# A second tile pool in a fused attention and gated-convolution kernel: every tile that TensorE reads gets one base address mod 256 bytes

## The chip, the core and the metric

The kernel runs on one core of one Trainium2 chip. The metric is device time in microseconds (us) of one execution, as the median of several runs. "Before" is the kernel without the change. Engines are called as the profile calls them: PE is TensorE's matmul side, PEld its weight load, DVE is VectorE, ACT is ScalarE, POOL is GpSimd, SP is the engine that issues the DMAs.

## What is computed

An attention between 512 tokens and 32 state vectors per head, both ways, whose two results are laid one behind the other along the sequence (544 rows), and on that a projection to 1024 columns, a convolution of three taps along the sequence, a gate, and a projection back. All in float32; B = 8, H = 8, D = 64.

```python
def attn(x, state):                              # x (8,8,512,64), state (8,8,32,64)
    a  = softmax(x @ state.T / 8)                # 512 x 32 for each head
    a2 = softmax(state @ x.T / 8)                # 32 x 512 for each head
    return concat([a @ state, a2 @ x], axis=2)   # 544 rows

def block(x, w_in, conv_w, w_out):               # x is (8, 544, 512) now
    h = maximum(x @ w_in, 0)                     # (8, 544, 1024)
    c = sum(conv_w[k] * shifted(h, k - 1) for k in range(3))
    return (h * sigmoid(c)) @ w_out              # (8, 544, 512)
```

## The kernel before

The work goes in eight batches `b`, and for each in eight slices `f` of 128 of the 1024 middle columns, which gives 64 steps `i`. The projection into the middle is not done as attention result times `w_in`: the state is multiplied by `w_in` first (`state_product`, L494, tile `u`), and a step is then `u` against the attention weights `a` (`hidden`, L579, out `ps_h`). ACT takes it out of PSUM through ReLU into `h` (L584), ACT and DVE make the three taps into `t` (L601, L605, L610), ACT the tanh of the gate (L614), DVE the gated product (L619). Then `t` is multiplied by `w_out` into four chunks of 128 rows (`project`, L637, out `acc`), which collect over the eight steps of a batch and are copied out by ACT or DVE (L651, L653) and stored. The 32 state rows of each batch go the same way in groups of four batches (`ps_hs`, `ss`, `gts`, `acc_t`), and one corner chunk is done late (`last`, `acc_c`).

Most products are done in a split form. A float32 tile is written by ACT as a rounded part (`high`, L178, type fp32r) and by DVE as the rest (`low`, L181), so the pairs `a0`, `a1`; `u0`, `u1`; `g0`, `g1`; the two halves of `wo`; `gts0`, `gts1` and the two parts of `last` come about. One product is then three fp32r matmuls of 512 columns: `PASSES = ((1, 0), (0, 1), (0, 0))`, rest times rounded, rounded times rest, rounded times rounded. In a matmul one operand is loaded as weights (128 columns) and the other streams by. In `project`, `tail` and `last_product`, all on L637, the slices of `g`, `gts` and `last` are loaded and `wo` streams; in `hidden`, `u` is loaded and `a` streams. The first batch and four of its steps run in plain float32, without a split (L574, L645).

`ORDER` is a table of numbers that sets the order of all operations by hand, on all engines; operations are not scheduled otherwise. What each waits for follows from the tiles that it reads and writes, and from how many buffers a tag has (`SBUF`).

Tiles of SBUF come from two pools. `keep` holds what stays for the whole run, in this order: `ident`, `cw`, `wi`, `wo`, `st`, `sr`, the 16 small `hs`, three `corner` tiles, `last`. `work` holds everything that is used in turn, through `buf` (L159 of before), a ring of buffers for each tag. The pools lie one behind the other in each partition, and in a pool the tags lie in the order in which they are first asked for, each rounded up to 32 bytes. So a tile whose size is no multiple of 256 bytes moves all that come after it to another place mod 256.

These are the places of the tiles in a partition, as the built program has them, mod 256 bytes. No base but those of the small tiles and of `h` differs within one row.

```
tile                       bytes     before   after
ident                        512        128     128
wi, wo, st, sr          2048-32768      224     128
last                        4096        192     128
xt, hc, at                2048-4096      192     128
a0 (streams in hidden)      4096         64     128
a1 (streams in hidden)      4096        192     128
u0 (loaded in hidden)       4096        192     128
u1 (loaded in hidden)       4096         64     128
the two parts of last       4096        192     128
xx, e2t, rr             512-4096        192     128
af, e2, t                2048-4096       64     128
g0, g1, gts0, gts1, ss     512-2048      64     128
o (copied out)              2048         64     128
h                           2052   192,224,0,32   192,224,0,32
hs, cw, corner, nm2, s1, s2   up to 544 bytes, at many places, the same mod 256 in both
```

`a0`, `a1` and `u1` share their buffers with `raw`, the tiles into which the weights are loaded at the start, and four of the last outputs share those of `xt` and `e2`.

Of the kernel before, what the change touches and what calls it, by code (L numbers as in the profile page):

```python
# [9 lines left out]
F32 = mybir.dt.float32  # L10
F32R = mybir.dt.float32r
# [4 lines left out]
P = 128  # L16
B, H, S, NS, D = 8, 8, 512, 32, 64
NP = H // 2
NG = H // 4
NCH = S // P  # L20
DM, DFF = 512, 1024
NK = DM // P
NF = DFF // P
T = S + NS

LOTS = ((0, 1, 2, 3), (4, 5, 6, 7))
# [16 lines left out]

SBUF = dict(hc=3, xt=4, xx=2, at=5, e2=2, e2t=2, af=1, a=2, u=2, h=4, t=5, g=4, ss=1,
            rr=2, nm2=4, s2=4, s1=4, o=2, gts=2)

RAW = ("a0", "a1", "u1")
PSUM = dict(acc=4, ph=2, ps=2)
# [103 lines left out]
def fused_kernel(ctx: ExitStack, tc: tile.TileContext, xT, xn, stT, w_in, conv_w, w_out, out):  # L152
    nc = tc.nc
    V, A, G, PE = nc.vector, nc.scalar, nc.gpsimd, nc.tensor

    psum = ctx.enter_context(tc.tile_pool(name="psum", bufs=4, space=bass.MemoryType.PSUM))
    keep = ctx.enter_context(tc.tile_pool(name="keep", bufs=1))
    work = ctx.enter_context(tc.tile_pool(name="work", bufs=2))

    def bank(name, tag="ps"):  # L160
        return psum.tile([P, 512], F32, tag=tag, name=name, bufs=PSUM[tag])

    def buf(shape, dtype, tag, name, pool=work, **kw):
        return pool.tile(shape, dtype, tag=tag, name=name, bufs=SBUF.get(tag) or SBUF[tag[:-1]], **kw)

    ident = keep.tile([P, P], F32, name="ident")
    make_identity(nc, ident)
    cw = keep.tile([P, NF, 3], F32, name="cw")
    wi = keep.tile([P, NK, DFF], F32, name="wi")
    wo = keep.tile([P, 2, NF, DM], F32R, name="wo")  # L170

    st = keep.tile([P, B * NP, NS], F32, name="st")

    sr = [keep.tile([P, NP, len(lot) * NS], F32, name=f"sr_{m}") for m, lot in enumerate(LOTS)]


    def high(hi, src):
# [24 lines left out]
    def w_tile(j, tag, *more):  # L202
        shape = [P, *pieces[j][0].shape[1:], *more]
        return buf(shape, U32, tag, f"{'raw' if more else tag}_{j}",
                   padded_shape=[P, *([1, 512] if j == W_CONV else shape[1:3]), *more])
# [18 lines left out]
    def w_sign(j):  # L224
        dst = pieces[j][1]
        if dst is None:
            f = j - W_OUT
            whole[f] = buf([P, DM], F32, f"g{f % 2}", f"whole_{f}")
            dst = whole[f].unsqueeze(1)
        V.scalar_tensor_tensor(dst.bitcast(U32), raws.pop(j)[:, :, :, 1], 0x80000000, hcs.pop(j),  # L230
                               op0=ALU.bitwise_and, op1=ALU.bitwise_or)
# [27 lines left out]
    at, ps_s, nm2, e2, ps_t, e2t, s2, ps_r, rr, ps_f, xts, xxs = ({} for _ in range(12))  # L259

    def xt_load(i):
        b, g = divmod(i, NG)
        xts[i] = buf([P, 2, S], F32, "xt", f"xt_{i}")
        nc.sync.dma_start(xts[i], xT[b, :, 2 * g:2 * g + 2, :])  # L264
# [99 lines left out]
    af, s1, av = {}, {}, {}  # L364
# [182 lines left out]
    corner = keep.tile([P, NF, 3], F32, name="corner")  # L547
    corner2 = keep.tile([P, NF, 3], F32, name="corner2")
    corners = keep.tile([P, 1, NF], F32, name="corners")
    last = keep.tile([P, NF, P], F32, name="last")  # L550

    def at_step(i):
        b, f = divmod(i, NF)
# [326 lines left out]
```

## Time and profile before

| | us |
|---|---|
| median of 3 runs | 376.81 |
| lowest and highest of them | 375.97, 378.32 |
| the profiled execution's own time | 376.16 |
| its span, first to last instruction | 374.4 |
| PE busy | 362.8 |
| DVE busy | 309.2 |
| ACT busy | 265.7 |
| POOL busy | 44.2 |

The granted clock of TensorE in the profiled execution was 0.996 of full speed. Busy time is the time that instructions of an engine cover, and PE's counts a matmul up to its modelled end, so that back-to-back matmuls overlap: the length of one matmul in a row is longer than the step from one to the next. The step is read from the chain of waits, which lists pieces of uninterrupted work with their length and the number of instructions in each.

### The profile page before, as it was taken

The page shows a single profiled execution, that of the slowest core. Times are in us where ns is not written, and L with a number is a line of the kernel's source. Part 1 is how long each engine was busy: PE and PEld are TensorE (multiplying, and loading weights), DVE is VectorE, ACT ScalarE, POOL GpSimd, SP SyncE. Part 2 cuts the span into 40 slices and gives each one's busy share as a digit, 9 for nine tenths or more (in the row PEclk, how much of TensorE's full clock was granted, in tenths as well). Part 3 has the DMA queues.
Part 4 walks back from the last instruction along what each step waited for, and adds up shares of the span by engine and source line. Part 5 has one row for each costly group of instructions (what it writes and reads, how often), then busy time and mean ns, then how long its engine had stood idle before and what let it go on. Part 6 is the DMA issues. An engine that isn't in the chain of part 4 may idle for free.

```text
span 374.4 us, 6509 instructions
## 1 busy us (share of the span) xinstructions
PE 362.8 (97%) x2418; PEld 267.4 (71%) x2418; DVE 309.2 (83%) x540; ACT 265.7 (71%) x536; POOL 44.2 (12%) x158
## 2 busy tenths in 40 slices
PE   7988989999999999999999999999999999999994
PEld 6852446677668776877888877877778778888883
DVE  1988999999999989989989898786787578666951
ACT  3898998866789689766765658666766477558632
POOL 1002102310121120102010011011311121011000
PEclk9999999999999999999999999999999999999998
DMA  7999984033310445000010011100020001002004
GB/s 257 326 355 312 379 290 166 0 114 100 141 43 2 144 141 190 34 2 4 28 56 2 0 56 58 56 4 15 13 86 0 28 30 56 2 0 86 3 0 168
DMA packets 21728, 35.05 MB, mean 94 GB/s; under 512 B 1600, under 2 KB 14272, under 8 KB 21696
## 3 DMA queue, kind: packets, MB, share of 16 engines
q1 hardware_dynamic: 21696, 34.63, 27.0%
q8 instruction: 19, 0.31, 0.4%
q14 instruction: 13, 0.11, 0.1%
HBM read 25.71 MB, written 8.91 MB: 92 GB/s over the span
## 4 chain that ended last, share of the span: by engine, by line
PE 89%; DMA 7%; SPq 2%; ACT 0%; issue 0%; ACTq 0%
PE acc L637 45%; PE ps_h L579 21%; PE ps_hs L560 4%; PE ps_u L494 4%; PE acc_t L637 3%; DMA raw<-w_in 3%; DMA st<-stT 3%; PE ps_h L574 2%; PE acc L645 2%; PE ps_r L318 2%; PE ps_s L277 2%; DMA xx<-xn 2%; PE acc_c L637 1%; PE ps_t L305 1%; SPq L209 1%; SPq L264 0%
## 5 line engine op out<-in xcount | busy, mean ns | idle before, releaser
L637 PE MATMUL acc<-wo,g 128*128 128x512 f32 x708 | 179.9, 400 | 0.0
L637 PEld LDWEIGHTS acc<-wo,g 128*128 128x128 f32 x708 | 131.0, 188 | 43.3 <-issue 8.4
L579 PE MATMUL ps_h<-a,u 128*128 128x512 f32 x336 | 85.7, 397 | 0.0
L579 PEld LDWEIGHTS ps_h<-a,u 128*128 128x128 f32 x336 | 62.4, 188 | 15.9 <-issue 1.7
L605 DVE SCALAR_TENSOR_TENSOR t<-h,cw,t 128x511 f32<-128x511 f32 x64 | 47.1, 744 | 11.0 <-ACT t L601 10.8
L584 ACT ACTIVATE h<-ps_h 128x512 f32<-128x512 f32 x64 | 37.8, 594 | 19.6 <-PE ps_h L579 12.9
L614 ACT ACTIVATE t<-t 128x512 f32<-128x512 f32 x64 | 39.6, 627 | 15.3 <-DVE t L610 15.2
L610 DVE SCALAR_TENSOR_TENSOR t<-h,cw,t 128x512 f32<-128x512 f32 (+1 forms) x64 | 47.3, 745 | 1.7 <-POOL h L589 0.5
L619 DVE SCALAR_TENSOR_TENSOR t<-t,h 128x512 f32<-128x512 f32 (+1 forms) x64 | 42.2, 666 | 5.8 <-ACT t L614 5.6
L181 DVE TENSOR_TENSOR g<-t,g 128x512 fp32r<-128x512 f32 (+1 forms) x60 | 40.2, 674 | 7.4 <-ACT g L178 7.1
L178 ACT ACTIVATE g<-t 128x512 fp32r<-128x512 f32 (+1 forms) x60 | 37.0, 621 | 11.9 <-DVE t L619 8.1
L601 ACT ACTIVATE t<-h,cw 128x512 f32<-128x512 f32 x64 | 44.7, 719 | 0.1
L589 POOL COPY h<-hs 128x1 f32<-128x1 f32 x56 | 20.3, 372 | 172.2 <-DVE t L619 141.9
L594 POOL COPY hs<-h 128x1 f32<-128x1 f32 x64 | 19.0, 315 | 120.3 <-ACT h L584 120.2
L651 ACT ACTIVATE o<-acc 128x512 f32<-128x512 f32 (+1 forms) x30 | 17.1, 584 | 11.6 <-PE acc L637 11.3
L181 DVE TENSOR_TENSOR u<-ps_u,u 128x512 fp32r<-128x512 f32 x28 | 18.6, 679 | 3.9 <-ACT u L178 3.9
L178 ACT ACTIVATE u<-ps_u 128x512 fp32r<-128x512 f32 x28 | 16.1, 594 | 4.2 <-PE ps_u L494 4.1
L188 PE MATMUL idle<-ident 128*128 128x128 f32 x102 | 14.8, 306 | 1.8 <-POOL ident masks.py:199 1.8
L560 PEld LDWEIGHTS ps_hs<-sr,wi 128*128 128x128 f32 x128 | 15.7, 191 | 1.2 <-ACT sr L333 0.4
L188 PEld LDWEIGHTS idle<-ident 128*128 128x128 f32 x102 | 13.7, 216 | 3.5 <-POOL ident masks.py:199 1.8
L213 ACT ACTIVATE hc<-raw 128x512 f32<-128x512 f32 (+1 forms) x17 | 11.1, 652 | 6.8 <-DMA raw<-conv_w 4.4
L560 PE MATMUL ps_hs<-sr,wi 128*128 128x128 f32 x128 | 15.7, 275 | 0.0
(88 smaller groups left out, 394.1 us busy)
## 6 DMA issues: line engine op xcount, KB each, us to landing
xt<-xT SPq DMA_DIRECT2D x16, 512.0 KB, 6.5
xx<-xn SPq DMA_DIRECT2D x16, 512.0 KB, 5.2
out<-o SPq DMA_DIRECT2D x30, 256.0 KB, 2.1
raw<-w_in SPq DMA_DIRECT2D x8, 512.0 KB, 7.1
raw<-w_out SPq DMA_DIRECT2D x8, 512.0 KB, 7.8
out<-o_t SPq DMA_DIRECT2D x8, 64.0 KB, 1.7
st<-stT SPq DMA_DIRECT2D x1, 448.0 KB, 10.4
out<-o_c SPq DMA_DIRECT2D x1, 256.0 KB, 6.7
```

What stands on the lines that cost most here:

```text
L178: A.activation(hi, src, AF.Copy)
L181: engine.tensor_tensor(lo, src, hi.bitcast(F32), op=ALU.subtract)
L188: PE.matmul(idle[0][:, :P], ident, ident, start=True, stop=True)
L560: PE.matmul(ps_hs[m, f][:, :NT], wi[:, k, f * P:(f + 1) * P], sr[m][:, k, :], start=(k == 0), stop=(k == NK - 1))
L579: PE.matmul(ps_h[i], u[j][:, g, fs], a[k][:, g, :], start=(n == 0), stop=(n == 3 * NG - 1))
L584: A.activation(hd[i][:, :S], ps_h.pop(i), AF.Relu, scale=0.5)
L601: A.activation(tt[i], hd[i][:, :S], AF.Copy, scale=cw[:, f, 1:2])
L605: V.scalar_tensor_tensor(t[:, 1:], h[:, :S - 1], cw[:, f, 0:1], t[:, 1:], op0=ALU.mult, op1=ALU.add)
L610: V.scalar_tensor_tensor(t[:, :n], h[:, 1:n + 1], cw[:, f, 2:3], t[:, :n], op0=ALU.mult, op1=ALU.add)
L614: A.activation(tt[i], tt[i], AF.Tanh, scale=0.25)
L619: V.scalar_tensor_tensor(tt[i][:, :n], tt[i][:, :n], 1.0, hd[i][:, :n], op0=ALU.add, op1=ALU.mult)
L637: PE.matmul(acc, g[j][:, cs], wo[:, k, f, :], start=(f == 0 and n == 0), stop=(f == NF - 1 and n == 2))
```

## The change

A third pool, `even`, is opened ahead of `keep` and `work`, and so lies first in each partition. Of the tiles that stay, `ident`, `wi`, `wo`, `st`, `sr` and `last` go there; `cw`, `hs` and the corner tiles remain in `keep`. Of the tiles used in turn, all go there but the four tags in `UNEVEN` (`h`, and three of 4 to 128 bytes), which remain in `work`. All sizes in `even` are multiples of 512 bytes, and the pool begins at byte 16512, which is 128 mod 256. So all its tiles begin there.

No instruction is added, removed or moved: on every engine the instructions of the two programs stand in the same order with the same operands, sizes and semaphore waits. Only the addresses differ, and the line numbers, which are 3 higher from the pools on. The number of buffers of each tag is the same.

```diff
+UNEVEN = ("h", "nm2", "s2", "s1")
 ...
+    even = ctx.enter_context(tc.tile_pool(name="even", bufs=1))
     keep = ctx.enter_context(tc.tile_pool(name="keep", bufs=1))
     work = ctx.enter_context(tc.tile_pool(name="work", bufs=2))
 ...
-    def buf(shape, dtype, tag, name, pool=work, **kw):
-        return pool.tile(shape, dtype, tag=tag, name=name, bufs=SBUF.get(tag) or SBUF[tag[:-1]], **kw)
+    def buf(shape, dtype, tag, name, **kw):
+        return (work if tag in UNEVEN else even).tile(shape, dtype, tag=tag, name=name, bufs=SBUF.get(tag) or SBUF[tag[:-1]], **kw)
 ...
-    ident = keep.tile([P, P], F32, name="ident")
+    ident = even.tile([P, P], F32, name="ident")
     make_identity(nc, ident)
     cw = keep.tile([P, NF, 3], F32, name="cw")
-    wi = keep.tile([P, NK, DFF], F32, name="wi")
-    wo = keep.tile([P, 2, NF, DM], F32R, name="wo")
+    wi = even.tile([P, NK, DFF], F32, name="wi")
+    wo = even.tile([P, 2, NF, DM], F32R, name="wo")
 ...
-    st = keep.tile([P, B * NP, NS], F32, name="st")
+    st = even.tile([P, B * NP, NS], F32, name="st")
 ...
-    sr = [keep.tile([P, NP, len(lot) * NS], F32, name=f"sr_{m}") for m, lot in enumerate(LOTS)]
+    sr = [even.tile([P, NP, len(lot) * NS], F32, name=f"sr_{m}") for m, lot in enumerate(LOTS)]
 ...
-    last = keep.tile([P, NF, P], F32, name="last")
+    last = even.tile([P, NF, P], F32, name="last")
```

## The prediction

> **What bounds the kernel now.** I read the page first, its shares and its chain of waits, and then the groups of the lines that the chain names. A group row gives the busy time in us, the mean ns of one instruction and, behind the bar, the idle time of the engine ahead of them.
>
> ```profile
> PE 362.8 (97%) x2418; PEld 267.4 (71%) x2418; DVE 309.2 (83%) x540; ACT 265.7 (71%) x536; POOL 44.2 (12%) x158
> ...
> PE 89%; DMA 7%; SPq 2%; ACT 0%; issue 0%; ACTq 0%
> PE acc L637 45%; PE ps_h L579 21%; PE ps_hs L560 4%; PE ps_u L494 4%; PE acc_t L637 3%; DMA raw<-w_in 3%; DMA st<-stT 3%; PE ps_h L574 2%; PE acc L645 2%; PE ps_r L318 2%; PE ps_s L277 2%; DMA xx<-xn 2%; PE acc_c L637 1%; PE ps_t L305 1%; SPq L209 1%; SPq L264 0%
> ...
> L637 PE MATMUL acc<-wo,g 128*128 128x512 f32 x708 | 179.9, 400 | 0.0
> L637 PEld LDWEIGHTS acc<-wo,g 128*128 128x128 f32 x708 | 131.0, 188 | 43.3 <-issue 8.4
> L579 PE MATMUL ps_h<-a,u 128*128 128x512 f32 x336 | 85.7, 397 | 0.0
> L579 PEld LDWEIGHTS ps_h<-a,u 128*128 128x128 f32 x336 | 62.4, 188 | 15.9 <-issue 1.7
> ```
>
> The reader is to see that PE itself is the bound: 89% of the chain that ended last is matmuls, ACT is on it with 0%, DVE not at all, and the 7% of DMA are loads. The fp32r matmuls of L637 and L579 alone make 45 + 21 + 3 + 1 = 70% of the chain. So what this change can do, it does in the step from one such matmul to the next. The 400 and 397 ns overlap and aren't that step. The chain in order of time gives it: start and length in us of each piece, and how many matmuls it has.
>
> ```profile
> 227.90 4.15 PE ps_h L579 x18
> ...
> 239.59 4.22 PE acc L637 x18
> ...
> 249.20 2.76 PE ps_h L579 x12
> 251.96 1.40 PE acc L637 x6
> ...
> 254.38 7.92 PE acc L637 x33
> 262.30 2.78 PE ps_h L579 x12
> ...
> 282.37 2.80 PE acc L637 x12
> 285.17 1.39 PE ps_h L579 x6
> 286.56 2.81 PE acc L637 x12
> ```
>
> Without the piece of 33, which has pauses in it, the 48 matmuls of `acc` take 4.22 + 1.40 + 2.80 + 2.81 = 11.23 us, a step of 234.0 ns. The 48 of `ps_h` take 4.15 + 2.76 + 2.78 + 1.39 = 11.08 us, 230.8 ns. Both stream 512 columns of fp32r against 128 loaded columns, and in both the weight load (188 ns) is shorter than the step and runs beside the stream before it. They differ by 3.1 ns, and they differ in place: `acc` streams `wo` from 224 mod 256 and loads `g` from 64. `ps_h` streams and loads at 64 and 192: rest `u1` and `a0` are both at 64, `u0` and `a1` both at 192, and only `u0` with `a0` is 128 apart. Two more pieces, from earlier, are needed below.
>
> ```profile
> 41.82 1.72 PE ps_h L574 x4
> ...
> 83.45 5.59 PE acc_c L637 x24
> ```
>
> `acc_c` streams the same `wo` as `acc` but loads from 192: 5.59 / 24 = 232.9 ns. So with all else alike, another place of the loaded operand goes with 1.1 ns. The plain float32 matmuls of L574 take 1.72 / 4 = 430 ns for the same 512 columns.
>
> **The change, part by part.** It removes, adds and moves no instruction; the order and the semaphores are the same on each engine. What is left is the address of every operand, and I go by engines.
>
> *fp32r matmuls.* All operands will be at 128, loaded and streamed alike, and all at the same distance as `u1` from `a0` and `u0` from `a1` now: none. The value 128 itself occurs in no fp32r matmul of this trace, so a bound has to do. The lower end is 215 ns, half of the 430 that the plain float32 pass takes for the same columns. The upper end is 240 ns, the 7.92 / 33 of the piece with pauses, for want of a slower clean one. The nearest row is `ps_h`, the one product whose operands already lie mostly at one place, so I take 230.8 ns. That changes nothing for the 336 matmuls of L579, and 3.1 to 3.2 ns for all that stream `wo`, 708 on the first row above and these:
>
> ```profile
> L637 PE MATMUL acc_t<-wo,gts 128*128 128x512 f32 x48 | 13.7, 400 | 0.0
> L637 PE MATMUL acc_c<-wo,last 128*128 128x512 f32 x24 | 5.8, 395 | 0.0
> ```
>
> (708 + 48 + 24) x 3.1 ns = 2.4 us. All of it lies on the path: 780 steps of 234 ns are 182.5 us, and the chain has 45 + 3 + 1 = 49% of 374.4 us, 183 us, on that line.
>
> *Plain float32 matmuls and transposes.* Their weight loads already show many places at one length:
>
> ```profile
> L560 PEld LDWEIGHTS ps_hs<-sr,wi 128*128 128x128 f32 x128 | 15.7, 191 | 1.2 <-ACT sr L333 0.4
> ...
> L574 PEld LDWEIGHTS ps_h<-p,u 128*128 128x128 f32 x32 | 5.6, 191 | 7.0 <-issue 6.6 <-ACT p L469 0.2
> ...
> L645 PEld LDWEIGHTS acc<-whole,t 128*128 128x128 f32 x24 | 3.8, 190 | 2.5 <-issue 2.3
> ```
>
> `sr` at 224, `u` at 192 and `t` at 64 all load in 190 or 191 ns, and the stream at 430 ns is far from that. I take nothing for them.
>
> *DVE and ACT.* The same helper runs on tiles at different places:
>
> ```profile
> L181 DVE TENSOR_TENSOR g<-t,g 128x512 fp32r<-128x512 f32 x56 | 38.1, 685 | 7.4 <-ACT g L178 7.1
> ...
> L178 ACT ACTIVATE g<-t 128x512 fp32r<-128x512 f32 x56 | 35.0, 628 | 11.5 <-DVE t L619 7.7 <-PE acc L637 3.6
> ...
> L181 DVE TENSOR_TENSOR wo<-whole,wo 128x512 fp32r<-128x512 f32 x8 | 5.3, 684 | 0.0
> ...
> L178 ACT ACTIVATE wo<-whole 128x512 fp32r<-128x512 f32 x8 | 5.0, 635 | 0.0
> ```
>
> `g<-t` reads and writes at 64 only, `wo<-whole` reads 64 and writes 224: 685 against 684 ns on DVE, 628 against 635 on ACT. Between nothing and 1% of an engine that isn't on the chain is nothing. What hides it is the matmul stream, and with 374.4 - 309.2 = 65 us free on DVE a stream that is 2.4 us shorter still does. If that cover went, `g` and `t` for L637 would be late next.
>
> *DMA.* The loads have only the place of their target changed, and 7% of 374.4 us, 26 us, of the chain are loads.
>
> ```profile
> xt<-xT SPq DMA_DIRECT2D x16, 512.0 KB, 6.5
> xx<-xn SPq DMA_DIRECT2D x16, 512.0 KB, 5.2
> ```
>
> Both targets are at 192, both carry 512 KB, and they differ by 1.3 us from issue to landing. A place can't be told from that, so I take nothing, and 1.3 us to either side as ends, for the last load that the chain waits for.
>
> The sum is -2.4 us: from the profiled execution's 376.16 us to 373.8. That execution is 0.65 us under the median of 376.81, so the same sum against the median gives **374.4 us**. One per cent, about what a measurement of this kernel can tell from no change, is 3.8 us, or 3.4 ns on each of 1116 fp32r steps, whose mean is now (780 x 234.0 + 336 x 230.8) / 1116 = 233.0 ns. So a mean under 229.6 would be faster by that measure, and one over 236.4 slower.
>
> **Rivals.** *Nothing happens.* The 3.1 ns then belong to the products and not to the places: which pass follows which, or that `wo` is another tensor in each pass while `a0` comes twice. For it speak the equal loads at 224, 192 and 64 above, against it `acc_c`, where the same passes go 1.1 ns faster. Time 376.8 us. The Trainium skill, "SBUF — State Buffer", sections "Specifications (TRN2)" and "Who interferes with whom", has lines of 16 bytes and one read port for the streamed operand and another for the weights, independent of each other. By that a base that is a multiple of 32, as all are in both programs, can't matter, the sum would be zero and the time 376.8; the 1.1 ns between `acc` and `acc_c` speak a little against it.
>
> *The reads stop disturbing each other.* The step has 233.0 - 215 = 18 ns above half the float32 pass. If a weight load and a stream that begin at one place never meet, up to all of that goes: 1116 x 18 ns = 20 us, 356.7 us. A third of it, 6 ns, gives 370.1. Against it: in `ps_h` two of three pairs already begin at one place and gain 3 ns, not 18. The Trainium skill, "TensorE: Matmul & The Clock Gate", section "Back-to-back issue gap", gives about 216 ns for 512 columns at full clock. By it the sum would be 1116 x 17 ns, 19 us less; the 430 ns of L574, twice 215, agree with the figure, the 233 here don't.
>
> *They meet each time.* The weight load begins when the stream before it begins. With both at one place mod 256, they ask for the same place of the memory at the same moment, in every step and not only in some, and each step pays for a meeting. At the 240 ns of the piece with pauses it would be 1116 x 7.0 ns = 7.8 us more, 384.6 us; it decides from 236.4 ns on. For it speaks only that no operand pair of L637 begins at one place now. Against it: `ps_h`, where two pairs of three do, is the fastest product here.
>
> **How the numbers follow.** The forecast, near `ps_h`'s step, has 0.45, nothing happens 0.30, reads that stop disturbing 0.14, reads that meet 0.11. The first two lie within 1%, and so does a small part of the other two, against which a small part of the first may go past 1%: faster 0.15, same 0.75, slower 0.10. The forecast's own range is 373 to 376. For 8 in 10 the range takes in no change with the spread of the runs (375.97 to 378.32), the 1.3 us of the loads and the beginnings of both outer cases: 371.0 to 380.0.
>
> **What would show it.** In the chain after, clean pieces of 12 and 18 `acc` matmuls at 2.77 and 4.15 us, as `ps_h` has them now, and those of `ps_h` unchanged, show the forecast right. Pieces at 2.80 and 4.22 show that places do nothing; 2.73 or less that the reads stopped disturbing each other; 2.84 or more that they meet. Weight loads at 188 and 191 ns, the helpers of L178 and L181 (three lines lower then) within 1%, and DMA at 7% show the parts at nothing right. What makes it wrong is an effect of 128 itself, which no fp32r operand has now, or the share of DMA moving.

## The result, and the profile after

| | before | after |
|---|---|---|
| median, us (8 runs each) | 377.02 | 374.36 |
| lowest and highest, us | 375.96, 381.54 | 371.31, 375.32 |
| ratio, 95% interval | | 0.9877 [0.9843, 0.9911] |
| the profiled execution's own time, us | 376.16 | 375.32 |
| its span, us | 374.4 | 373.5 |

The kernel got faster by 1.2%, with an interval that begins at 0.9%, while its medians alone give 0.993. A second measurement of the same kernel, below, gives 0.9913 [0.9876, 0.9950]. So the gain is about one per cent, at the line that the prediction drew for what can be told from no change. The profiled execution of the changed kernel is its slowest (375.32 of 371.31 to 375.32).

From the page of the changed kernel, shares, chain and groups (its lines are 3 higher):

```profile
PE 358.2 (96%) x2418; PEld 266.2 (71%) x2418; DVE 309.0 (83%) x540; ACT 265.9 (71%) x536; POOL 43.0 (12%) x158
...
PE 65%; DVE 16%; DMA 10%; ACT 5%; issue 3%; SPq 1%; DVEq 0%; ACTq 0%
PE acc L640 33%; PE ps_h L582 16%; DMA st<-stT 4%; PE ps_u L497 4%; DMA xx<-xn 4%; PE ps_hs L563 2%; PE ps_s L280 2%; DVE t L613 2%; DMA raw<-w_out 2%; DVE g L184 2%; DVE t L608 2%; PE ps_r L321 2%; DVE t L622 2%; PE acc L648 1%; PE acc_t L640 1%
...
L640 PE MATMUL acc<-wo,g 128*128 128x512 f32 x708 | 176.2, 395 | 0.1
L640 PEld LDWEIGHTS acc<-wo,g 128*128 128x128 f32 x708 | 130.5, 188 | 40.9 <-issue 8.4
L582 PE MATMUL ps_h<-a,u 128*128 128x512 f32 x336 | 84.4, 393 | 0.0
L582 PEld LDWEIGHTS ps_h<-a,u 128*128 128x128 f32 x336 | 62.3, 188 | 14.7 <-issue 1.7
```

PE's busy time fell by 4.6 us though the number of its instructions is the same, and the chain changed its make: PE went from 89% to 65%, and DVE came up from nothing to 16%. The weight loads kept their 188 ns.

The chain of waits after, in order of time, with start and length in us and the number of matmuls of each piece, over the stretch that the prediction used:

```profile
229.84 4.08 PE ps_h L582 x18
...
241.30 4.08 PE acc L640 x18
...
250.72 2.72 PE ps_h L582 x12
253.44 1.36 PE acc L640 x6
...
255.81 7.72 PE acc L640 x33
263.54 2.72 PE ps_h L582 x12
...
283.16 2.72 PE acc L640 x12
285.88 1.36 PE ps_h L582 x6
287.24 2.72 PE acc L640 x12
```

Every piece of this list but the one of 33, which has pauses, is now at 226.7 ns a matmul (4.08 / 18, 2.72 / 12, 1.36 / 6), and `acc` and `ps_h` no longer differ. Before, they were at 234.0 and 230.8. By these pieces the matmuls should have saved 780 x 7.3 + 336 x 4.1 = 7.1 us. That takes the best pieces for all. From the start times in the trace, the mean step from one fp32r matmul to the next of its kind, over all that follow without a pause, went from 233.9 to 227.9 ns for those that stream `wo` and from 232.0 to 227.7 ns for `ps_h`. By these means the matmuls saved 780 x 6.0 + 336 x 4.3 = 6.1 us, an estimate that takes the steps across a pause to have gained as much. The clock is no part of it: from 75 to 366 us the granted clock is 1.00 in the profile of either kernel and of every one below.

The span shows less, and the chains tell at which two places. First the start. The chain of before, in order of time:

```profile
47.42 6.18 DMA xx<-xn
...
63.42 7.14 PE ps_hs L560 x64
...
72.44 1.60 PE acc L637 x6
```

And of after:

```profile
49.01 7.03 DMA xx<-xn
...
57.54 6.46 DMA xx<-xn
...
66.72 7.14 PE ps_hs L563 x64
...
75.74 1.58 PE acc L640 x6
```

The first fp32r matmul comes 3.3 us later, because two loads of `xx` end late on the chain where before there was one. From there to the end of the span it is 374.4 - 72.44 = 302.0 us before and 373.5 - 75.74 = 297.8 after: 4.2 us less, not 6.1. The second place, where about 2 us are lost, is the middle of the run. The chain between 180 and 222 us, by line, first before and then after:

```profile
by line: PE acc L637 50.1%; PE ps_h L579 20.0%; PE ps_hs L560 17.0%; PE acc_t L637 13.4%
```

```profile
by line: issue 12.2%; DVE g L184 7.7%; DVE ss L683 7.3%; DVE t L613 6.7%; DVE t L608 6.5%; DVE t L622 6.1%; DVE af L402 5.6%; DVE af L381 5.5%; PE acc L640 4.9%; DVE s L395 4.9%; DVE m L385 4.7%; DVE at L405 3.0%; DVE af L388 2.8%; PE ps_hs
```

What was all matmuls is now mostly DVE: the shares of DVE in what is shown of this line add up to 61%. That DVE took the gain there is tested at the end of the experiments.

### The profile page after: what moved, and what is told of

Same layout as the page of the kernel before. It is cut to its first block, busy times and chain, and to the rows that moved or that the text cites. A ratio compares the mean times of both kernels' runs of the same rounds, so it can differ in the third digit from the quotient of the medians.

```text
span 373.5 us, 6509 instructions
## 1 busy us (share of the span) xinstructions
PE 358.2 (96%) x2418; PEld 266.2 (71%) x2418; DVE 309.0 (83%) x540; ACT 265.9 (71%) x536; POOL 43.0 (12%) x158
## 4 chain that ended last, share of the span: by engine, by line
PE 65%; DVE 16%; DMA 10%; ACT 5%; issue 3%; SPq 1%; DVEq 0%; ACTq 0%
PE acc L640 33%; PE ps_h L582 16%; DMA st<-stT 4%; PE ps_u L497 4%; DMA xx<-xn 4%; PE ps_hs L563 2%; PE ps_s L280 2%; DVE t L613 2%; DMA raw<-w_out 2%; DVE g L184 2%; DVE t L608 2%; PE ps_r L321 2%; DVE t L622 2%; PE acc L648 1%; PE acc_t L640 1%
## 5 line engine op out<-in xcount | busy, mean ns | idle before, releaser
L640 PE MATMUL acc<-wo,g 128*128 128x512 f32 x708 | 176.2, 395 | 0.1
L582 PE MATMUL ps_h<-a,u 128*128 128x512 f32 x336 | 84.4, 393 | 0.0
L597 POOL COPY hs<-h 128x1 f32<-128x1 f32 x64 | 17.7, 295 | 120.6 <-ACT h L587 118.4
L563 PEld LDWEIGHTS ps_hs<-sr,wi 128*128 128x128 f32 x128 | 15.5, 191 | 2.2 <-ACT hs L567 1.2
L563 PE MATMUL ps_hs<-sr,wi 128*128 128x128 f32 x128 | 15.9, 276 | 0.4 <-ACT hs L567 0.3
```

The lines of the kernel that those rows point to most:

```text
L563: PE.matmul(ps_hs[m, f][:, :NT], wi[:, k, f * P:(f + 1) * P], sr[m][:, k, :], start=(k == 0), stop=(k == NK - 1))
L582: PE.matmul(ps_h[i], u[j][:, g, fs], a[k][:, g, :], start=(n == 0), stop=(n == 3 * NG - 1))
L640: PE.matmul(acc, g[j][:, cs], wo[:, k, f, :], start=(f == 0 and n == 0), stop=(f == NF - 1 and n == 2))
```

## The experiments

Theory one, the "one-place" theory: what counts is the distance, mod 256 bytes, between the operand that is loaded and the one that streams. The rival, the "line" theory: each operand counts for itself, by its place against a line of 128 or 256 bytes of the memory. 128 and not 64 or 224 would then be the good place. All kernels but two below compute the whole result.

The table has the clean pieces of 12 matmuls from the chain of each profile, and the time from the start of the first fp32r piece to the end of the span. That last column leaves the start out. The ratio is to the kernel before, run beside it; mixD ran only twice, so its ratio says little and its steps have to speak for it.

```
kernel       wo,g apart  a,u apart     12 acc   12 ps_h  first fp32r to end   ratio, 95%
before           160     0,128,0      2.80-2.81 2.76-2.78      302.0
changed            0        0            2.72      2.72        297.8          0.9877 [0.9843, 0.9911]
again              0        0            2.72      2.72        297.8          0.9913 [0.9876, 0.9950]
all0               0        0            2.72      2.72        297.7          0.9905 [0.9864, 0.9946]
all64              0        0            2.72      2.72        297.9          0.9920 [0.9869, 0.9970]
all224             0        0            2.72      2.72        297.8          0.9904 [0.9864, 0.9945]
mixA              96       64            2.79    2.79-2.80     301.5          0.9988 [0.9946, 1.0031]
mixB              64      192         2.76-2.79  2.79-2.80     300.2          0.9953 [0.9913, 0.9992]
mixC             128      128         2.79-2.80  2.78-2.80     301.4          1.0028 [0.9981, 1.0075]
mixD        256 (0 mod 256) both         2.72      2.72        297.7          0.9880 [0.9715, 1.0046]
wo_only            0     0,128,0      2.73-2.76  2.77-2.79     299.3          0.9926 [0.9893, 0.9959]
rest128     128 in one pass of three     2.77      2.77        299.8          0.9961 [0.9927, 0.9996]
```

**The same kernel again**, with no edit.

> The changed kernel once more. Both theories: clean pieces of 12 fp32r matmuls at 2.72 us for acc and for ps_h, ratio to before near 0.988. Open: whether the loads at the start again cost some 3 us more than in the profile of before (if the places of the targets do it, they do here too; if it is chance, the start may be as in before).

The pieces came out at 2.72 us, and the start was late once more: its first fp32r piece begins at 75.92 us. That alone would make one think that the places of the load targets cost it. The next kernels settle that.

**All tiles at another place.** One line ahead of all tiles of `even`, with 32, 48 or 24 columns:

```diff
     even = ctx.enter_context(tc.tile_pool(name="even", bufs=1))
+    even.tile([P, 32], F32, name="pad")
```

> The whole pool begins 128 bytes later, so that all tiles in it lie at 0 mod 256 in place of 128. One-place theory (only the distance between the loaded and the streamed operand matters): 12 matmuls in 2.72 us, time as the changed kernel. Line theory (each operand's place against a line of 128 bytes matters): the same, 2.72 us; if the line is 256 bytes, faster, 2.68 us or less, some 3 us less in all.

> All tiles of the pool at 64 mod 256. One-place theory: 12 matmuls in 2.72 us, time as the changed kernel. Line theory: both operands are off the line again, 2.77 us or more for acc and ps_h, 3 to 5 us slower than the changed kernel.

> All tiles of the pool at 224 mod 256, where wo lay before. One-place theory: 12 matmuls in 2.72 us, time as the changed kernel. Line theory: 2.80 us or more, also for ps_h, and a time at or over that of the kernel before (375 to 378 us).

The chain of the kernel with all at 64, in order of time:

```profile
72.34 1.58 PE acc L641 x6
...
247.34 2.72 PE ps_h L583 x12
...
279.79 2.72 PE acc L641 x12
```

And with all at 224, where `wo` lay before:

```profile
73.67 1.59 PE acc L641 x6
...
248.65 2.72 PE ps_h L583 x12
...
281.08 2.72 PE acc L641 x12
```

And with all at 0:

```profile
73.49 1.60 PE acc L641 x6
...
248.43 2.72 PE ps_h L583 x12
...
280.87 2.72 PE acc L641 x12
```

One length at all four places: the line theory is out. 128 has nothing of its own; 0, a multiple of 256, gains nothing more, and 64 and 224 lose nothing.

**Operands at chosen distances.** Extra pools with a pad hold some of the tiles, here as in the first of them:

```diff
+    p1 = ctx.enter_context(tc.tile_pool(name="p1", bufs=1))
+    p1.tile([P, 24], F32, name="pad_p1")
+    p2 = ctx.enter_context(tc.tile_pool(name="p2", bufs=1))
+    p2.tile([P, 24], F32, name="pad_p2")
 ...
-        return (work if tag in UNEVEN else even).tile(...
+        return (p2 if tag in ('u0', 'u1') else work if tag in UNEVEN else even).tile(...
 ...
-    wo = even.tile([P, 2, NF, DM], F32R, name="wo")
+    wo = p1.tile([P, 2, NF, DM], F32R, name="wo")
```

> As the changed kernel, but wo streams from 224 mod 256 (96 from what it is multiplied with) and u0, u1 are loaded from 64 (64 from a). One-place theory: 12 matmuls of acc and of ps_h are back near 2.80 us, 376 to 378 us in all. Line theory, already weak: acc slow, ps_h slow too. Start of the kernel: if the place of the load targets costs the 3 us, the first fp32r matmul comes at 78 us as in the changed kernel's profiles, since xx and xt lie at 128 here too.

> As the changed kernel, but the other operands are moved: g0, g1 are loaded from 64 mod 256 while wo streams from 128, and a0, a1 stream from 64 while u is loaded from 128; acc_t and acc_c keep both at 128. One-place theory: acc and ps_h near 2.80 us for 12, acc_c at 24 in 5.44 us as in the changed kernel. If only the streamed operand mattered, acc would stay at 2.72; if only the loaded one, ps_h would.

> As the changed kernel, but wo, u0 and u1 lie at 0 mod 256, so that loaded and streamed operand are 128 bytes apart in every matmul of acc and ps_h. One-place theory with a period of 256: 2.80 us or more for 12, both; this is also the greatest distance, so perhaps the slowest. With a period of 128 bytes: 2.72 us.

> As the changed kernel, but wo, u0 and u1 lie 256 bytes further: all at 128 mod 256 still, but 256 apart mod 512. One-place theory with a period of 256 bytes (what the change is named after): 2.72 us for 12, time as the changed kernel. With a period of 512 bytes: 2.80 us.

The chain of the first, with `wo` 96 and `u` 64 bytes away from their partners:

```profile
73.07 1.59 PE acc L644 x6
...
84.03 5.60 PE acc_c L644 x24
...
249.67 2.79 PE ps_h L586 x12
...
282.86 2.79 PE acc L644 x12
```

Of the second, where the other operand of each pair was moved and `acc_c` was left at one place:

```profile
75.91 1.59 PE acc L642 x6
...
86.89 5.46 PE acc_c L642 x24
...
251.95 2.80 PE ps_h L584 x12
...
284.89 2.79 PE acc L642 x12
...
289.08 2.76 PE acc L642 x12
```

Of the third, 128 apart everywhere, and of the fourth, 256 apart:

```profile
250.71 2.80 PE ps_h L584 x12
...
283.86 2.79 PE acc L642 x12
```

```profile
72.18 1.59 PE acc L642 x6
...
247.14 2.72 PE ps_h L584 x12
...
279.58 2.72 PE acc L642 x12
```

Moving the streamed operand, or the loaded one, undoes most or all of the gain; `acc_c`, whose operands stayed together in the second kernel, keeps 5.46 us against 5.60 in the first. At 64 to 192 bytes apart the loss is about the same, with some 3 ns between the least (mixB's `acc`) and the rest (mixB, with 300.2 us, keeps some of the gain). At 256 it is gone: the period is 256 bytes, not 128 and not 512. The expectation that 128 apart would perhaps be the slowest did not hold.

The start is settled too. In the changed kernel, its repetition, the four kernels here and the last of this series, the targets `xt` and `xx` lie at 128, and the first fp32r piece begins at 75.74, 75.92, 73.07, 75.91, 74.24, 72.18 and 74.62 us. It varies by 3.7 us with the place unchanged. And in the kernels below that keep `xt` and `xx` where they were before, `wo_only` and the one before without a tap, it begins at 75.54 and 74.85 us, against 72.44 in the profile of before. So the place of these targets does not make the start late. (One expectation gives 78 us for the changed kernel; its profile has 75.74.) What decides when those loads end is open.

**`wo` alone**, in the kernel before:

```diff
+    keep.tile([P, 24], F32, name="pad")
     wo = keep.tile([P, 2, NF, DM], F32R, name="wo")
+    keep.tile([P, 40], F32, name="pad2")
```

> The kernel before with wo alone moved, to 64 mod 256, where g and gts lie; every other operand is where it was. One-place theory: 12 matmuls of acc in 2.72 us (227.5 ns a step), acc_t likewise, acc_c (128 apart) and ps_h as before at 233 and 231.8 ns; a ratio to before of some 0.991 to 0.995, a part of what the whole change gives. If it takes all tiles at one place, acc stays at 234 and the ratio is 1.00.

```profile
75.54 1.59 PE acc L639 x6
...
86.49 5.59 PE acc_c L639 x24
...
264.11 2.79 PE ps_h L581 x12
...
283.96 2.73 PE acc L639 x12
```

One tile of the kernel, moved by 96 bytes, gives 2.7 of the 4.2 us, and `acc` goes alone: `ps_h` and `acc_c` stay where they were. But the 12 matmuls of `acc` take 2.73 to 2.76 us and not 2.72. By the start times, the first three steps of a row of `acc` matmuls take 231.2 ns here on average, the next six 229.2, and from the tenth on 226.9; in the changed kernel it is 228.5, 228.5 and 226.9. In mixB the tail product `acc_t`, whose operands lie at one place but which comes in rows of 3 or 6 among disturbed `acc`, takes 230.1 ns a step, against 226.9 in the changed kernel. So the distance of a matmul's own operands isn't all that counts; it looks as if what ran just before carries over for some matmuls. That, and why, is not shown.

**One operand of three passes apart.** `g1` and `u1` in a pool that begins 128 bytes off; nothing else differs from the changed kernel.

> The changed kernel with the loaded rests g1 and u1 alone 128 bytes apart from all else. If the load is disturbed by the stream that runs beside it, only the step of the third pass is longer (while it streams, the next rest is loaded), 235 ns or more against 227.5 for the other two. If the operands of one matmul with each other decide it, the step of the first pass is longer. If the stream before and after a load count as well, two or all three are longer.

From the start times in the trace, the mean step from each pass to the next, over 142 products of `acc` and 59 of `ps_h` that have another of their kind behind them without a pause:

```
                                  acc      ps_h
pass 1 to 2 (loaded: apart)      233.8    233.7 ns
pass 2 to 3                      227.5    227.5
pass 3 to 1 (loading: apart)     232.3    232.2
```

Two of three steps are long: the one while the operand that lies apart is loaded beside a stream, and the one in which it is then used. The third is free of it. So it's not the load beside the stream alone, as the simplest form of the theory had it. Nor does this rule explain each step of `ps_h` in the kernel before. There `u0` is apart from `a0`, beside which it is loaded in pass 1 and with which it is used in pass 3, while `u0` and `a1` are together, so the step from pass 2 to 3 should be free of it. The same count gives 231.9, 233.3 and 230.8 ns. Why is open; there the streams change place from pass to pass too.

**Where the rest of the gain went.** The third tap of the convolution on DVE is left out, in the kernel before and in the changed one. The outputs lack that tap.

```diff
     def behind(i):
         f, h, t = i % NF, hd[i], tt[i]
         n = S if i >= NF else S - 1
-        V.scalar_tensor_tensor(t[:, :n], h[:, 1:n + 1], cw[:, f, 2:3], t[:, :n], op0=ALU.mult, op1=ALU.add)
```

> The kernel before without the third tap of the convolution on DVE (64 operations of 745 ns, 47.7 us of DVE time; the output lacks that tap). With after_less it tells where the rest of the step's gain went. If DVE absorbed it in the middle of the run: from the first fp32r matmul to the last this kernel takes 6 us or more longer than after_less. If something else did: the difference stays at the 4.1 us of the whole kernels.

> The changed kernel without the third tap of the convolution on DVE (the output lacks that tap). If DVE absorbed gain: 6 us or more under before_less from the first fp32r matmul to the last, and chain of waits with hardly any DVE. If something else did: 4.1 us under it.

The ratios to the kernel before are 1.0033 [0.9995, 1.0070] and 0.9858 [0.9809, 0.9907]. The first fp32r piece begins at 74.85 us of a span of 376.8, and at 74.01 of 370.0:

```profile
74.85 1.60 PE acc L636 x6
```

```profile
74.01 1.60 PE acc L639 x6
```

That leaves 302.0 us without the tap in the old places, as with it, and 296.0 in the new ones: 6.0 us less, in place of 4.2. The shares of the chain without the tap, in the new places:

```profile
PE 87%; DMA 8%; DVE 3%; SPq 1%; issue 0%; ACT 0%; DVEq 0%
```

DVE has gone from 16% to 3%, and PE is back at 87%. So with the matmuls in the old places 41 us less DVE work is worth nothing, and in the new ones 1.8 us: there DVE had taken that much of the gain. And the 6.0 us are what the mean steps of all fp32r matmuls give, 6.1.

## Why the prediction came out as it did

The time, 374.4 us, is that of the measured median, and it lies inside the range. That is luck: the terms behind it do not stand so well.

*What bounds the kernel, and what the change is.* Right: the same instructions, and a shorter step of the fp32r matmuls on the path.

*The price of the step.* This is the term that was mis-sized. "The nearest row is `ps_h`, the one product whose operands already lie mostly at one place, so I take 230.8 ns." Measured was 226.7 in the clean pieces of both, and 227.9 and 227.7 on the mean of all steps. Two pairs of three at one place are not two thirds of the gain: the run with one operand of three passes apart has two long steps of three. So `ps_h` was itself disturbed, "that changes nothing for the 336 matmuls of L579" fell with it (they gave 1.4 us of the 6.1), and the sum for the steps was 2.4 us where it should have been 6.1. The rival in which "the reads stop disturbing each other" had the better picture: its "a third of it" of the 18 ns, 6 ns, is what came, on the step of the clean pieces from 233.0 to 226.7, and the sign that the prediction named for it, pieces of 12 at 2.73 us or less, is what the chain shows. It had 0.14, and was marked down by the very row that misled.

*DVE and ACT hide it.* "With 374.4 - 309.2 = 65 us free on DVE a stream that is 2.4 us shorter still does." For 2.4 us perhaps, for 6 not, and the free time was taken over the whole span where it should have been read by stage. In the stretch from 80 to 220 us DVE had been nearly full before already; the columns are the stretch, its length, the busy us of PE, PEld, DVE, ACT and POOL, and at the end the granted clock, the DMA share and GB/s:

```profile
80.00:220.00 140.00, 140.00 (x976) 107.03 (x976) 131.37 (x219) 103.23 (x212) 16.09 (x53) 1.00 0.20 67
220.00:370.00 150.00, 149.60 (x717) 114.14 (x715) 109.67 (x183) 96.75 (x183) 17.78 (x56) 1.00 0.10 37
```

131.4 of 140 us leaves 8.6 us, not 65. What would be late next was named in part: `t` and `g` are on the new chain, and so are the `ss` and `af` tiles.

*Plain float32, DVE and ACT lengths, at nothing.* Right: weight loads of L560 (L563 after) at 191 ns on either page, the two taps on DVE at 744 to 746 ns each, and four plain matmuls of L574 (L577 after) in 1.72 us on either chain.

*DMA at nothing, 1.3 us to either side.* Nothing is right for the place. The ends were too narrow for what the loads do by themselves: the start varies by 3.7 us, and the share of DMA on the chain went from 7% to 10%, which the prediction had named as a sign of being wrong.

So the gain in the matmuls was two and a half times the forecast, 6.1 against 2.4 us, and DVE took it down to 4.2; a step gain taken too small and a cover taken too wide worked against each other. The medians, of executions that are spread over 4.0 us after and 5.6 us before, moved by 2.7 us; that this comes so near the 2.4 of the forecast is chance. Of the two measurements one, 0.9877, is past the one per cent that the prediction took as its line, and one, 0.9913, short of it.

*The two rules that the prediction cited.* By "SBUF — State Buffer", sections "Specifications (TRN2)" and "Who interferes with whom" of the Trainium skill, a base that is a multiple of 32 bytes could not matter, since the two read ports are independent. The runs decide against that for fp32r: 226.7 ns at one place mod 256, about 233 at 96 or 128 apart. The about 216 ns that the Trainium skill gives in "TensorE: Matmul & The Clock Gate", section "Back-to-back issue gap", was not reached as a mean at any place that was tried: 226.7 ns was the least.

## What to carry to other kernels

Where fp32r matmuls of 512 columns each bring their own weights, put the loaded and the streamed operand at one base mod 256 bytes: it costs a pad and gave 2 to 3% on the step. Which place they share made no difference at the four that were tried, and one tile may be most of it: moving the one that most matmuls stream gave 2.7 of 4.2 us. Other types and widths were not tried. Read the cover of another engine by stage before a gain is counted: here DVE with 65 us free over the span had 8.6 free where it counted, and took back 1.8 of 6.0 us.

## What was not expected of the hardware

The distance of two read-only operands changes the step of a matmul with a period of 256 bytes: 226.7 ns in clean pieces at 0 and 256 apart, 230 to 234 at 32, 64, 96, 128, 160 and 192. What it is in the chip that does this, no run here shows. Where one operand of three passes lay apart, it cost in two steps, while it was loaded and while it was used (232.3 and 233.8 against 227.5 ns); the steps of `ps_h` in the kernel before do not follow that rule. And where `wo` alone was moved, and `ps_h` stayed disturbed, a row of `acc` matmuls at one place began at 231.2 ns a step and came to 226.9 from the tenth on. The loads at the start let the first fp32r matmul begin up to 3.7 us apart in programs whose `xt` and `xx` have the same place.
